# A fused gated-convolution kernel, forward and backward: order of the first slice, loading of k, buffers of gate and up, and replacement of the gradient pieces

## The chip, the cores and the metric

The kernel runs on one core of a Trainium2 chip. Its engines are TensorE (PE; its weight loads are listed as PEld), VectorE (DVE), ScalarE (ACT), GpSimd (POOL) and SyncE (SP). SP issues most of the transfers; ScalarE and GpSimd issue some too, each from its own instruction stream. The metric is the device time of one execution in microseconds. Before the change, nine runs have a median of 1946.38 us (1940.92 to 1960.81).

## The reference

All inputs are bf16. A sequence of 2048 rows by 1024 columns goes through a layer norm, and two branches use the result: a gated long convolution, and a bilinear unit with F = 3584. The kernel computes the output and the gradients of nine of the inputs (out_0 to out_9).

```python
xn = _layernorm(A_q)
# branch A: a short filter of 4 taps on k, times v, a long filter by FFT, gated by xn
k_shift = sum_t  k_pad[:, t:t + S, :] * shift_k[:, ks - 1 - t]
kv = k_shift * v
y  = irfft(rfft(kv, 2S) * rfft(ssm_k, 2S))[:S] + kv * ssm_D
s  = xn * y
# branch B
g = xn @ w_gate; u = xn @ w_up
g = silu((g * u) @ w_down)
out = A_q + s * g
# and the vector-Jacobian product of out with grad_out for
# q, k, v, shift_k, ssm_k, ssm_D, w_gate, w_up, w_down
```

## The kernel before, in words

The work runs in five stages, which one can tell by the line of TensorE's matmuls.

*Startup and forward.* `layer_norm` normalizes 2048 rows in six chunks and turns them into XNT (U0 to U3). `gu_unit(sl, b0, n, w, tick)` makes n blocks of 128 rows of gate and up for one slab of 256 columns of F: eight matmuls a block (L635), a copy from PSUM to `gut` by ScalarE (L637), a store of `gut` to GUd issued by ScalarE (L642), then the product hN on VectorE (L646), its store to Hd through GpSimd's queue, the turn of hN by TensorE (L656), a copy by ScalarE and a store to HTd. The pool `fg` has two buffers of `gut`.

Between the blocks lies the long convolution, `conv_forward`, a generator. `tick` counts blocks and calls `pump`, which runs the generator forward to a given fraction of `F_TOTAL`; that is how its work is dealt out among the matmuls. The convolution goes over eight slices of 128 columns. For each pair of slices `shift` makes kv from k (with a halo of three rows), v and the taps, on VectorE. k arrives in two steps: `copy_k` copies 256 columns of k to a scratch tensor KSLd through SP's queue (rows of its own, three zero rows ahead of them, written by `zero_rows`), and `cld_k` loads it from there, eleven rows for each partition in one piece, through GpSimd's queue. For each slice, `half` transforms kv and the filter by matmuls with the tables T4 (L235), ScalarE copies the result to SP tiles (L257, L295), and VectorE does the rest (`transform`): first kv's spectrum KX, then the filter's HX, their `product`, and the inverse. `h_rows` turns the filter's rows, which `load_h` puts into the first half of U5. From L778 on VectorE keeps the order in which the code issues (`PIN`).

*Gates.* L949 multiplies by w_down; `gate` makes the output and the gradients that go further back. *Weight gradients.* L1302 and L1319 by slabs, then L1395 for w_down, with h loaded from Hd by `load_h` (L1334); the backward convolution (`conv_backward`, which starts with the forward transforms of dy in `dy_forward`) is dealt out among these by `bpump` on VectorE.

*Input gradient* (L1447). The gradient of xn from branch B is a sum over 14 pieces n; a piece is `ts[n]`, 512 rows of dg or du in 128 x 4 x 512, loaded transposed by `load_dgut` (L1385) in two transposing transfers on SP's queue. The 16 row blocks make four groups of four. In the first group every piece is used for all four blocks; in the later ones two passes, b = 4g and 4g + 2, go over all pieces for two blocks each. Every pass fills two tiles `psx` of PSUM, of which there are four. `ln_backward` reads them on VectorE (L1478), goes on with the gradient through the layer norm, and stores a block of the result. In the same stage `dk_units` makes the gradients of k and of the taps on VectorE; it loads k and its gradient transposed (kT, dkT, L1119 and L1121) on SP's queue as well, and each of these has one buffer. The pieces of the next group go into the same buffers (`gd`, `gd2`, one each) as those being used.

Queues keep order: a transfer on SP that waits for TensorE or VectorE holds up those behind it.

Of the kernel before, what the change touches and what calls it, by code (L numbers as in the profile page):

```python
# [13 lines left out]
BF16 = mybir.dt.bfloat16  # L14
# [5 lines left out]
def build_kernel(  # L20
# [55 lines left out]
    def cld_k(t, c, dp):  # L76

        src = KSLd[dp]
        cld(t, bass.AP(src.tensor, src.offset + 1024 * c * 256, [[8 * 256, P], [256, 11], [1, 256]]))

# [21 lines left out]
    KSHd = dram.tile([4, P, NB, 256], BF16, name="KSHd")  # L102
    KSLd = dram.tile([4, S + 8, 256], BF16, name="KSLd")
    DYd = dram.tile([8, P, NB, P], BF16, name="DYd")
# [4 lines left out]
    GUd = dram.tile([NSL, 2, P, 2, 8, SLW], BF16, name="GUd")  # L109
    Hd = dram.tile([NSL, P, NB, SLW], BF16, name="Hd")  # L110
    HTd = [[dram.tile([n, S // 2], BF16, name=f"HTd{i}{n}") for n in (24 * P, 4 * P)] for i in range(2)]
# [23 lines left out]
    def zero_rows(bsb):  # L135
        zr = bsb.tile([8, 8, P], BF16, name="zr")
        V.memset(zr[:], 0.0)
        st(KSLd[:, 0:3, :], zr[0:4].rearrange("p a x -> p (a x)")[:, 0:768].rearrange("p (a x) -> p a x", a=3))
        st(DKSHd[:, S:S + 8, :], zr[:])
# [387 lines left out]
    Dz = kst.tile([P, D], BF16, name="Dz")  # L527
    V.memset(Dz[:], 0.0)
    bsb = pool("bc_sb", 1)
    tg = pool("tg", 1)  # L530
# [82 lines left out]
    def flush(age=0):  # L613
# [3 lines left out]
        while later and later[0][0] >= age:  # L617
            later.pop(0)[1]()

    hn = [nop]  # L620
    chunk = [0]

    def gu_unit(sl, b0, n, w, tick):

        if n == 4:
            gut = fg.tile([P, 2, 4, SLW], BF16, name="gut")
            hN = fg.tile([P, 4, SLW], BF16, name="hN", bufs=3)
        else:
            gut = lnp.tile([P, 2, 2, SLW], BF16, name="gut_s", bufs=6)
            hN = lnp.tile([P, 2, SLW], BF16, name="hN_s", bufs=6)  # L630
        for i in range(n):
# [12 lines left out]
        def multiply():  # L644
            with tc.issue_after(last.ins) if b0 + n <= 4 and chunk[0] <= 2 else nullcontext():
                tt(hN[:, 0:n], gut[:, 0, 0:n], gut[:, 1, 0:n], MUL)  # L646
            st(Hd[sl][:, b0:b0 + n, :], hN[:, 0:n])
            defer(turn)
        hn[0] = multiply

        def turn():
            hT = fg.tile([P, 2, 4, P], BF16, name="hT") if chunk[0] > 5 else lnp.tile([P, 2, 4, P], BF16, name="hT_s", bufs=5)
            ps = ps_tr.tile([P, 2, 4, P], BF16, name="tr")
            for a in range(2):
                for i in range(n):
                    nc.tensor.transpose(ps[:, a, i, :], hN[:, i, a * P:(a + 1) * P], ident[:])  # L656
            nc.scalar.copy(out=hT[:, :, 0:n], in_=ps[:, :, 0:n])
            fr, so = sl % 12 * SLW, b0 % 8 * P
            ld(HTd[b0 // 8][sl // 12][fr:fr + SLW, so:so + n * P].rearrange("(a f) s -> f a s", f=P),
               hT[:, :, 0:n].rearrange("f a i s -> f a (i s)"))  # L660

# [7 lines left out]
    def conv_forward():  # L669
        S_ = conv_state  # L670

        def load_kv(dp, c):
            if c == 0:
                S_["k", dp] = kst.tile([P, 2, 11, 256], BF16, name="k")
            cld_k(S_["k", dp][:, c], c, dp)
            v = U[4][:, 2048 * c:2048 * c + 2048].rearrange("p (a x) -> p a x", a=8)
            cld_v(v, c, dp * 256, 256)

# [104 lines left out]
        tl = turn_tables(ps_y)  # L783
        sp = [half(0, kvs(0), i) for i in range(2)]
        for ds in range(8):
            yield 0.5
            if ds % 2 == 1 and ds < 7:
                with tc.issue_after(S_["kst"].ins):
                    for c in range(2):
# [4 lines left out]
            HX = cs.tile([P, 16, 256], BF16, name="HX", bufs=2)  # L794
            room = HX[:].rearrange("p a x -> p (a x)").bitcast(F32).rearrange("p (a x) -> p a x", a=8)[:, 0:4]
            yield from transform(ds, 0, sp, KX, room, lambda i: sph.append(half(ds, S_["hx"], i, D0)), nop)
            S_["kst"] = st(KFd[ds], KX[:])
            next(tl, None)
            eight = (ds, 1) in EIGHT
            room = cf.tile([P, 4, 256], F32, name="room", tag="hx")[:] if eight else None  # L800
            yield from transform(ds, 1, sph, HX, room, nop1 if eight else lambda c: h_rows(ds + 1, c),
                                 lambda: next(tl, None))
            if eight:
                h_rows(ds + 1, 0)
# [40 lines left out]

    def copy_k(dp):
        ld(KSLd[dp, 3:3 + S, :].rearrange("(p a) d -> p a d", a=16),
           kin[:, dp * 256:(dp + 1) * 256].rearrange("(p a) d -> p a d", a=16))
    copy_k(0)
    ang, ang_ins = angles(tg)  # L850
# [43 lines left out]
    def tick(by=1):  # L894
        cnt[0] += by
        if cnt[0] == -2:
            pump((SHIFT_W + 3.95) / F_TOTAL)
        if cnt[0] >= 0:
            pump((SHIFT_W + (F_TOTAL - SHIFT_W) * (cnt[0] + 5) / (NT + 2)) / F_TOTAL)

    pump(SHIFT_W / F_TOTAL)
    for i_ in (4, 5):
        gu_unit(1, *xs[i_][0:2], slabs[1], tick)
    for sl in range(2, NSL - 2):
        w, wld = load_slab(sl, nc.sync)
        if sl in (2, 4, 6):
            with tc.issue_after(wld.ins):
                copy_k(sl // 2)
        for hf in range(2):
            for b0 in (8 * hf, 8 * hf + 4):  # L910
                gu_unit(sl, b0, 4, w, tick)
# [70 lines left out]
    def dy_forward(xs_, sp, cs, then):  # L982
# [10 lines left out]
        load(1)  # L993
        yield 7.0
        half(0, 0)
# [161 lines left out]

    C_TOTAL = 7.0 + 8 * FWD8_W + 16 * (PROD_W + INV8_W) + 8 * 1.4 + 8 * 2.5
    bpump, bdrain = make_pump(conv_backward(), C_TOTAL)
# [174 lines left out]
    def load_h(sl):  # L1334
        h = u8(HSL[sl % 3], "p (b f) -> p b f", b=NB)
        ld(h, Hd[sl])
        hs[sl] = h
# [46 lines left out]

    def load_dgut(g, n):  # L1385

        a, j = pieces[n]
        t = (gd2 if n < 4 else gd).tile([P, 4, 512], BF16, name=f"dgut{n}")
        for i in range(2):
            nc.sync.dma_start_transpose(out=t[:, 2 * i:2 * i + 2], in_=DGd[2 * j + i, a, 512 * g:512 * g + 512, :])  # L1390
        return t

    def dwd_mm(ps, h, f, dh):
        for b in range(NB):
            nc.tensor.matmul(ps, h[:, b, f * P:(f + 1) * P], DBM[b // 4][:, b % 4, dh * 512:(dh + 1) * 512],  # L1395
                             start=(b == 0), stop=(b == NB - 1))
# [101 lines left out]
    for n in range(12):  # L1498
        for i in range(4):
            dx_part(ts, i, pss[i], n)  # L1500
        ts[n] = load_dgut(1, n)
    for i in range(4):
        for n in (12, 13):
            dx_part(ts, i, pss[i], n)
        if i == 3:
            for n in (12, 13):
                ts[n] = load_dgut(1, n)
        with tc.high_priority(40):
            ln_backward(i, pss[i][:])
    for g in range(1, 4):  # L1510
        for b in (4 * g, 4 * g + 2):
            end = b == NB - 2
            pss = [ps_x.tile([P, D], F32, name="psx") for i in range(2)]
            for n in range(12 if end else 14):
# [5 lines left out]
                if end and n == 4:  # L1520
                    h = u8(2, "p (b f) -> p b f", b=NB)
                    ld(h, Hd[NSL - 1])
                if end and n == 8:
                    ln_loads(NB - 1)
                if b % 4 == 2 and not end:
                    ts[n] = load_dgut(g + 1, n)
            if end:
# [81 lines left out]
```

## Time and profile before

| | |
|---|---|
| median of nine runs | 1946.38 us (1940.92 to 1960.81) |
| the profiled execution | 1960.81 us, span 1959.0 us |
| TensorE busy | 1923.8 us, 98% |
| VectorE busy | 1543.8 us, 79% |
| ScalarE busy | 638.4 us, 33% |
| GpSimd busy | 310.0 us, 16% |
| mean granted TensorE clock | 0.995 |
| moved by DMA | 448.62 MB, mean 229 GB/s |

The profile is of one execution, and its time is one of the nine. A busy engine is one with an instruction running; transfers count for none of them. "Idle before" an instruction is the time that its engine stood still, with what ended that. The granted clock is the share of full speed that TensorE was given; where it is 0.50, a matmul takes twice as long. The timeline joins neighbouring instructions of the same kind (x16 is sixteen of them).

### The profile page before, as it was taken

How to read it: one execution, taken by the hardware profiler on the slowest of the kernel's cores; microseconds unless marked ns; L12 is line 12 of the kernel's file. 1: busy time of each engine (PE TensorE's matmuls, PEld its weight loads, DVE VectorE, ACT ScalarE, POOL GpSimd, SP SyncE). 2: the span in 40 equal slices, each digit the busy share in tenths (PEclk: the TensorE clock that was granted, in tenths of full speed). 3: DMA queues.
4: the chain of work that ended last, by engine and by line, in shares of the span. 5: the costliest groups of instructions: out<-in, count | busy, mean ns of one | idle time of the engine just before them, and what ended most of it. 6: DMA issues, size and time to landing. Idle time of an engine off the chain costs nothing.

```text
span 1959.0 us, 27347 instructions
## 1 busy us (share of the span) xinstructions
PE 1923.8 (98%) x10994; PEld 1033.6 (53%) x10994; DVE 1543.8 (79%) x1719; ACT 638.4 (33%) x942; POOL 310.0 (16%) x454
## 2 busy tenths in 40 slices
PE   8999999999999999999999999999999999998989
PEld 4555555555544447665666665654444444443434
DVE  9999999999837556887899999999994405677673
ACT  5854555555422224342222222222212002001122
POOL 4111111101112220001022221211212002111111
PEclk9999999999999999999999999999999999999999
DMA  9886856657879987656788697585889999897993
GB/s 311 283 262 220 285 200 211 233 205 253 285 221 315 306 281 269 220 203 213 265 249 265 219 265 257 180 281 176 244 221 193 138 203 224 145 182 157 192 197 131
DMA packets 457071, 448.62 MB, mean 229 GB/s; under 512 B 266916, under 2 KB 377576, under 8 KB 442480
## 3 DMA queue, kind: packets, MB, share of 16 engines
q1 hardware_dynamic: 401168, 247.55, 49.0%
q0 software_dynamic: 39456, 169.96, 26.9%
q10 hardware_dynamic: 16320, 29.36, 4.1%
q8 instruction: 86, 1.41, 0.3%
q14 instruction: 41, 0.34, 0.1%
HBM read 198.20 MB, written 189.84 MB: 198 GB/s over the span
## 4 chain that ended last, share of the span: by engine, by line
PE 72%; DVE 9%; DMA 7%; issue 3%; SPq 2%; ACT 1%; POOL 0%; DVEq 0%; ACTq 0%; POOLq 0%
PE psb L1319 20%; PE psb L1302 10%; PE psbm L949 10%; PE psb L1395 9%; PE psg L635 9%; PE psx L1447 8%; PE psF L235 3%; SPq L1390 2%; DMA GUd<-gut 1%; DVE W L213 1%; DVE dkp L1148 1%; DVE U L213 1%; DMA HTd<-hT 1%; DVE KX L213 1%; DMA xn_t<-XNd 1%
## 5 line engine op out<-in xcount | busy, mean ns | idle before, releaser
L635 PE MATMUL psg<-wslab,U 128*128 128x512 bf16 x1792 | 409.9, 380 | 5.2 <-ACT gut L637 2.7
L1319 PE MATMUL psb<-U,U 128*128 128x512 bf16 x1792 | 397.4, 379 | 0.0
L1447 PE MATMUL psx<-U,dgut 128*128 128x512 bf16 x1536 | 338.0, 382 | 10.8 <-DMA dgut<-DGd 10.8
L1447 PEld LDWEIGHTS <-dgut 128*128 128x128 bf16 x1792 | 176.0, 98 | 226.8 <-DMA dgut<-DGd 13.5
L1319 PEld LDWEIGHTS <-U 128*128 128x128 bf16 x1792 | 175.3, 98 | 197.5
L635 PEld LDWEIGHTS <-U 128*128 128x128 bf16 x1792 | 173.3, 98 | 192.2 <-issue 7.5
L1302 PE MATMUL psb<-wdt,U 128*128 128x256 bf16 x1792 | 205.3, 273 | 0.0
L1302 PEld LDWEIGHTS <-U 128*128 128x128 bf16 x1792 | 175.3, 98 | 30.7
L637 ACT CAST gut<-psg 128x512 bf16<-128x512 f32 x216 | 125.9, 587 | 182.5 <-PE psg L635 162.0
L1395 PE MATMUL psb<-U,U 128*128 128x512 bf16 x816 | 177.1, 379 | 0.0
L213 DVE TENSOR_TENSOR W<-W 128x1024 f32<-128x1024 f32 (+1 forms) x168 | 168.8, 1022 | 3.6
L1324 ACT CAST wb<-psb 128x512 bf16<-128x512 f32 x112 | 65.6, 585 | 311.1 <-PE psb L1319 292.7
L949 PE MATMUL psbm<-U,ht 128*128 128x512 bf16 x672 | 145.7, 379 | 0.0
L1395 PEld LDWEIGHTS <-U 128*128 128x128 bf16 x896 | 87.4, 98 | 104.6
L1479 ACT ACTIVATE dx_t<-dxn 128x1024 bf16<-128x1024 f32 x15 | 15.9, 1057 | 336.3 <-DVE dxn L213 336.3
L949 PEld LDWEIGHTS <-ht 128*128 128x128 bf16 x672 | 65.6, 98 | 78.6
L1304 ACT CAST dht<-psb 128x512 bf16<-128x512 f32 x112 | 65.5, 585 | 120.2 <-PE psb L1302 119.0
L213 DVE TENSOR_TENSOR U<-U,dht 128x2048 bf16<-128x2048 bf16 x56 | 68.2, 1220 | 44.7 <-ACT dht L1304 44.6
L213 DVE TENSOR_TENSOR dxn<-psx,dxna_t 128x1024 f32<-128x1024 f32 x15 | 18.3, 1222 | 98.6 <-PE psx L1447 84.4
L1148 DVE SCALAR_TENSOR_TENSOR dkp<-dkT,kT 128x1024 bf16<-128x1024 bf16 (+2 forms) x64 | 78.3, 1224 | 19.2 <-DMA dkT<-DKSHd 17.3
L1426 ACT CAST wbs<-psb 128x512 bf16<-128x512 f32 x51 | 29.9, 585 | 146.4 <-PE psb L1395 137.0
L213 DVE TENSOR_TENSOR W<-SP 128x1024 f32<-128x1024 f32 x64 | 74.2, 1218 | 2.9 <-ACT SP L295 2.4
(249 smaller groups left out, 2368.8 us busy)
## 6 DMA issues: line engine op xcount, KB each, us to landing
U<-GUd SPq DMA_DIRECT2D x28, 1024.0 KB, 7.8
DGd<-U SPq DMA_DIRECT2D x28, 1024.0 KB, 4.4
GUd<-gut ACTq DMA_DIRECT2D x54, 512.0 KB, 6.2
out_dram<-wb SPq DMA_DIRECT2D x112, 128.0 KB, 4.0
U<-Hd SPq DMA_DIRECT2D x14, 1024.0 KB, 5.7
Hd<-hN POOLq DMA_DIRECT2D x54, 256.0 KB, 5.3
HTd<-hT SPq DMA_DIRECT2D x52, 256.0 KB, 3.9
ht<-HTd SPq DMA_DIRECT2D x6, 1536.0 KB, 11.5
```

Of the source, the lines that this page charges most:

```text
L213: pinned(V.tensor_tensor(o, a, b, op))
L235: mm = nc.tensor.matmul(ps[:, k].rearrange("p (c d) -> p c d", c=2), T[:, r, k, :], xr[:, r], start=(n == 0), stop=(n == len(rs) - 1 and ( ...
L635: gu_mm[0] = nc.tensor.matmul(ps[:], XNT[q][:, dc, qi * P:(qi + 1) * P], w[:, dc].rearrange("p a f -> p (a f)"), start=(dc == 0), stop=(dc ...
L637: nc.scalar.copy(out=gut[:, :, i], in_=ps[:].rearrange("p (a f) -> p a f", a=2))
L949: mm = nc.tensor.matmul(ps[:, dh * 512:(dh + 1) * 512], ht(fc)[:, i * P:(i + 1) * P], WD[fc // 4][:, fc % 4, dh * 512:(dh + 1) * 512], sta ...
L1148: ins = V.scalar_tensor_tensor(prod[:].rearrange("p r d -> p (r d)")[:, lo:H], dkT[:, 0, lo:H], 1.0, kT[:, 0, 13 + m + lo:13 + m + H], op0 ...
L1302: nc.tensor.matmul(ps[:, x * SLW:(x + 1) * SLW], DBMT[2 * hf + g][:, dc, (b % 4) * P:(b % 4 + 1) * P], wdt[:, dc, :], start=(dc == 0), sto ...
L1304: nc.scalar.copy(out=dht[:, 2 * e:2 * e + 2].rearrange("p b f -> p (b f)"), in_=ps[:])
L1319: nc.tensor.matmul(ps[:], XN[b // 4][:, b % 4, dc * P:(dc + 1) * P], dgus[b // 8][:, :, b % 8], start=(b == 0), stop=(b == NB - 1))
L1324: nc.scalar.copy(out=wb[:, dc % 2].rearrange("p a f -> p (a f)"), in_=ps[:])
L1395: nc.tensor.matmul(ps, h[:, b, f * P:(f + 1) * P], DBM[b // 4][:, b % 4, dh * 512:(dh + 1) * 512], start=(b == 0), stop=(b == NB - 1))
L1447: nc.tensor.matmul(ps[:, dh * 512:(dh + 1) * 512], t[n][:, f, i * P:(i + 1) * P], WGU[n][:, f, dh * 512:(dh + 1) * 512], start=(n == 0 and ...
```

## The change

It has four parts and some edits that go with them.

1. *Forward, first slice.* The filter is transformed ahead of kv: `sp` is filled from hx, HX is made first (with KX as room), then KX. The pump is called earlier, so that `h_rows` stands ahead of the first unit after the startup.
2. *k.* `cld_k` reads k from the input itself, eleven rows of 512 bytes for each partition. The first half of the sequence takes three loads (partitions 16 to 127, 1 to 15, and 0, which has three rows less), since row -3 to -1 do not exist; they are set to zero once in a single tile `krow`, which all pairs of slices use. KSLd, `copy_k` and its calls go. For the first pair both halves of k are loaded ahead of both of v.
3. *gate and up.* Every third unit of four blocks puts `gut` into the second half of U5 (not in the last two slabs). hN and Hd hold the two halves of a slab's columns one after the other; the product reads `gut` in that order, and `dwd_mm` reads h in it.
4. *Gradient pieces.* `load_dgut` can load one half, 256 rows, into an existing tile. In groups 1 and 2 each pass asks, after each piece, for that half of the next group's piece whose columns this pass has just used. The first group's loads stay whole.

The backward convolution's first half is dealt out four units later (`yield 11.0`, `C_TOTAL`).

```diff
     def cld_k(t, c, dp):
-        src = KSLd[dp]
-        cld(t, bass.AP(src.tensor, src.offset + 1024 * c * 256, [[8 * 256, P], [256, 11], [1, 256]]))
+        rows = lambda u, n, a: bass.AP(kin.tensor, kin.offset + (1024 * c + 8 * u - 3 + a) * D + dp * 256,
+                                       [[8 * D, n], [D, 11 - a], [1, 256]])
+        for u, n, a in ((0, P, 0),) if c else ((16, P - 16, 0), (1, 15, 0), (0, 1, 3)):
+            cld(t[u:u + n, a:], rows(u, n, a))
...
+    krow = kst.tile([P, 2, 11, 256], BF16, name="k")
+    V.memset(krow[0:1, 0, 0:3, :], 0.0)
...
         if n == 4:
-            gut = fg.tile([P, 2, 4, SLW], BF16, name="gut")
-            hN = fg.tile([P, 4, SLW], BF16, name="hN", bufs=3)
+            turn_of[0] += 1
+            if turn_of[0] % 3 == 0 and sl < NSL - 2:
+                gut = U[5][:, 2048:4096].rearrange("p (a i f) -> p a i f", a=2, i=4)
+            else:
+                gut = fg.tile([P, 2, 4, SLW], BF16, name="gut")
+            hN = fg.tile([P, 2, 4, P], BF16, name="hN", bufs=3)
...
-                tt(hN[:, 0:n], gut[:, 0, 0:n], gut[:, 1, 0:n], MUL)
-            st(Hd[sl][:, b0:b0 + n, :], hN[:, 0:n])
+                by_half = lambda t: t.rearrange("p i (a f) -> p a i f", a=2)
+                tt(hN[:, :, 0:n], by_half(gut[:, 0, 0:n]), by_half(gut[:, 1, 0:n]), MUL)
+            st(Hd[sl][:, :, b0:b0 + n, :], hN[:, :, 0:n])
...
         def load_kv(dp, c):
-            if c == 0:
-                S_["k", dp] = kst.tile([P, 2, 11, 256], BF16, name="k")
-            cld_k(S_["k", dp][:, c], c, dp)
-            v = U[4][:, 2048 * c:2048 * c + 2048].rearrange("p (a x) -> p a x", a=8)
-            cld_v(v, c, dp * 256, 256)
+            S_["k", dp] = krow
+            if dp > 0 or c == 0:
+                for i in range(2) if dp == 0 else (c,):
+                    cld_k(krow[:, i], i, dp)
+            if dp > 0 or c == 1:
+                for i in range(2) if dp == 0 else (c,):
+                    v = U[4][:, 2048 * i:2048 * i + 2048].rearrange("p (a x) -> p a x", a=8)
+                    cld_v(v, i, dp * 256, 256)
...
-        sp = [half(0, kvs(0), i) for i in range(2)]
+        sp = [half(0, S_["hx"], i, Dz[:, 0:P]) for i in range(2)]
...
-            yield from transform(ds, 0, sp, KX, room, lambda i: sph.append(half(ds, S_["hx"], i, D0)), nop)
-            S_["kst"] = st(KFd[ds], KX[:])
+            own_room = lambda X: X[:].rearrange("p a x -> p (a x)").bitcast(F32).rearrange("p (a x) -> p a x", a=8)[:, 0:4]
+            eight = (ds, 1) in EIGHT
+            if ds == 0:
+                yield from transform(0, 1, sp, HX, own_room(KX), lambda i: sph.append(half(0, kvs(0), i)), nop)
+            else:
+                yield from transform(ds, 0, sp, KX, own_room(HX), lambda i: sph.append(half(ds, S_["hx"], i, D0)), nop)
+                S_["kst"] = st(KFd[ds], KX[:])
...
-        if cnt[0] == -2:
-            pump((SHIFT_W + 3.95) / F_TOTAL)
+        if cnt[0] == -4:
+            pump((SHIFT_W + 4.05) / F_TOTAL)
...
-    pump(SHIFT_W / F_TOTAL)
+    pump((SHIFT_W + 3.95) / F_TOTAL)
...
-        if sl in (2, 4, 6):
-            with tc.issue_after(wld.ins):
-                copy_k(sl // 2)
...
-        yield 7.0
+        yield 11.0
...
-    def load_dgut(g, n):
+    def load_dgut(g, n, t=None, h=None):
         a, j = pieces[n]
-        t = (gd2 if n < 4 else gd).tile([P, 4, 512], BF16, name=f"dgut{n}")
+        if t is None:
+            t = (gd2 if n < 4 else gd).tile([P, 4, 512], BF16, name=f"dgut{n}")
+        r0, r1 = (0, 512) if h is None else (256 * h, 256 * h + 256)
         for i in range(2):
-            nc.sync.dma_start_transpose(out=t[:, 2 * i:2 * i + 2], in_=DGd[2 * j + i, a, 512 * g:512 * g + 512, :])
+            nc.sync.dma_start_transpose(out=t[:, 2 * i:2 * i + 2, r0:r1], in_=DGd[2 * j + i, a, 512 * g + r0:512 * g + r1, :])
...
-                if b % 4 == 2 and not end:
-                    ts[n] = load_dgut(g + 1, n)
+                if g < 3:
+                    load_dgut(g + 1, n, ts[n], b % 4 // 2)
```

## The prediction

> **What bounds the kernel now.** I read the page first, then TensorE's waits, then busy time by stage, then the timeline around each gap.
>
> ```profile
> span 1959.0 us, 27347 instructions
> PE 1923.8 (98%) x10994; PEld 1033.6 (53%) x10994; DVE 1543.8 (79%) x1719; ACT 638.4 (33%) x942; POOL 310.0 (16%) x454
> ```
>
> TensorE is busy for 98% of the span, and the change leaves its 10994 matmuls as they are. Only idle TensorE time, and time at a lower clock, can be won. The busy time by stage (startup, forward, gates, weight gradients, input gradient) says where that lies; the columns are stretch, length, busy time of PE, PEld, DVE, ACT, POOL, granted clock, DMA share, GB/s.
>
> ```profile
> 0.00:60.00 60.00, 51.32 (x393) 29.88 (x394) 54.94 (x154) 35.35 (x56) 24.21 (x42) 1.00 0.95 325
> 60.00:500.00 440.00, 428.13 (x2647) 238.78 (x2646) 420.36 (x372) 248.31 (x347) 59.98 (x98) 0.99 0.70 235
> 500.00:733.00 233.00, 232.86 (x1164) 110.62 (x1163) 146.27 (x209) 69.94 (x81) 43.50 (x68) 1.00 0.92 284
> 733.00:1538.80 805.80, 805.74 (x4941) 472.25 (x4940) 691.04 (x664) 225.45 (x375) 125.13 (x151) 1.00 0.76 229
> 1538.80:1941.50 402.70, 391.86 (x1794) 175.99 (x1792) 223.49 (x314) 52.00 (x74) 56.04 (x94) 0.98 0.95 185
> ```
>
> TensorE idles 8.7 us in the startup, 11.9 in the forward stage, 10.8 in the input-gradient stage (L1447), and nothing to speak of between. The clock is below 1.00 in the same two later stages. Where:
>
> ```profile
> 1772.79 1.89 PE L1447 MATMUL psx<-U,dgut 128*128 128x512 bf16 x4 [2.60 <-DMA dgut<-DGd]
> 1776.49 4.97 PE L1447 MATMUL psx<-U,dgut 128*128 128x512 bf16 x16 [1.81 <-DMA dgut<-DGd]
> 1782.06 3.19 PE L1447 MATMUL psx<-U,dgut 128*128 128x512 bf16 x14 [0.59 <-DMA dgut<-DGd]
> ...
> 1876.99 7.21 PE L1447 MATMUL psx<-U,dgut 128*128 128x512 bf16 x22 [5.84 <-DMA dgut<-DGd]
> ...
> 191.71 3.27 PE L235 MATMUL psF<-kv,TF 128*128 128x256 bf16 x16 [2.27 <-DVE kv L213]
> ...
> 308.82 1.91 PE L235 MATMUL psF<-kv,TF 128*128 128x256 bf16 x16 [0.93 <-DVE kv L213]
> ...
> 353.77 1.89 PE L635 MATMUL psg<-wslab,U 128*128 128x512 bf16 x8 [1.26 <-ACT gut L637]
> ...
> 396.68 1.67 PE L635 MATMUL psg<-wslab,U 128*128 128x512 bf16 x7 [1.24 <-ACT gut L637]
> ```
>
> And what follows three of these gaps (same columns as above; the clock is the third number from the right):
>
> ```profile
> 192.06:195.47 3.41, 3.41 (x17) 2.23 (x15) 3.38 (x3) 1.46 (x2) 0.00 (x0) 0.50 0.48 192
> ...
> 1772.43:1779.26 6.83, 4.66 (x11) 1.48 (x12) 1.39 (x2) 3.17 (x5) 0.54 (x1) 0.50 1.20 206
> 1874.83:1881.66 6.83, 4.67 (x11) 1.65 (x12) 4.00 (x5) 2.50 (x5) 1.61 (x3) 0.50 1.22 214
> ```
>
> **The clock, row against rule.** After these gaps the clock stands at 0.50, so half of the busy time there is lost too: 1.7 us after the kv gap, 2.3 after each dgut gap. The Trainium skill (TensorE: Matmul & The Clock Gate, Part 1) says that the clock is halved after an idle window of about 3.4 us. Read as "a gap must last that long", only the 5.84 gap would cost clock, and the change would gain 1.7 + 2.3 = 4.0 us less. The trace halves it after 2.27 and 2.60 us. I take the row. A fourth halving at 492.4 (1.7 us) follows a wait that the change doesn't touch, so the stage sums are: startup 8.7, forward 11.9 + 3.4 = 15.3, input gradient 10.8 + 4.7 = 15.5, together 39.5 us.
>
> **Part 1: gradient pieces in halves.** A pass over two row blocks is 224 matmuls, 48.4 us at 0.216 each (112 in 24.34). Before, the pieces for the next group of four blocks are asked for only in the second pass: 28 transposes, each due 45 us after its piece is freed. The queue can't keep that: the 28 issues for the third group begin at 1697.6 and end at 1781.6, since each holds SP for 2.42 us on average (1.22 at best) and key transposes stand between them waiting for VectorE:
>
> ```profile
> 1697.61 25.68 SPq L1390 DMA_TRANSPOSE dgut<-DGd  x10
> 1728.35 1.19 SPq L1119 DMA_TRANSPOSE kT<-in_A_k_dram  x1
> ```
>
> After, a half (256 rows) is asked for in each pass and due 97 - 3 = 94 us later. The four waits are 0.6 to 5.8 us long against a notice of 45, so doubled notice covers them. The waits in the built order are per half, so no pass waits for the other half. *Rule against it:* DMA: Bandwidth & Descriptors (Latency and other measured facts) gives transposing DMAs 261 GB/s with a strided middle dimension. A 256 KB piece would take 1.0 us, 28 would be through in 28 us, and lateness would need another cause, for which halving is worth 0. The trace has 2.42 us, 108 GB/s; I take it.
>
> The price is issues: 112 half pieces instead of 56 whole ones. A half-size transpose isn't in the trace. Below it is half of 1.22 (0.6 us); above, the whole's own stretched 2.42. The nearest row is a whole at rest, 1.22 to 1.31; I take 1.0. A pass then holds SP 28 x 1.0 plus 3.5 key pairs x 2.5 = 37 us of 48.4. Gain: 15.5, the whole stage loss.
>
> What is late next is psx. VectorE frees it in an order fixed by its own chain, and it never waits for TensorE here. The last pass began at 1941.5 - 48.4 = 1893.1; without the stalls it begins at 1877.6 and its second block needs its bank at 1879.3. VectorE reads that bank here:
>
> ```profile
> 1880.31 1.23 DVE L213 TENSOR_TENSOR dxn<-psx,dxna_t 128x1024 f32<-128x1024 f32 x1
> ```
>
> It ends at 1881.5: 2.2 us late if VectorE's chain keeps its time. That chain will move both ways. In SP's new order, 14 halves stand ahead of the key transpose that came directly after the second group's pieces (1673.55), so it goes out 14 us later, and VectorE, which waited 7.8 us there, waits more. Its later waits for dkT, dxna_t, xn_t and the dka store from 1714 on sum to some 36 us, and arise in bursts of whole pieces which now spread over two passes; if half goes, 18 is won back. Net cost between 0 and 14; I take 1.
>
> **Part 2: the first slice's filter first.** VectorE ends kv at 74.7, then idles 1.58 and 2.39 us for the copies of kv's transform. The filter needs neither k nor v, so its copies are ready and VectorE gains 2.4 to 4 us. The kv gap (2.27 + 1.7 clock) and the 0.93 one end on VectorE, 95% busy in this stage, so a lead there shortens them: at most 4.9; at least the lead of 2.4. I take 4.9, because closing the 2.27 gap also spares the clock.
>
> **Part 3: third gate/up buffer.** ScalarE waits 17.7 us in 7 places for the store of gut; two reach TensorE, 1.26 + 1.24 = 2.5. The third buffer lies in the free half of U5, so nothing is queued behind it. Gain 2.5 (at least 0, if the store's own lateness grows).
>
> **Part 4: k's rows straight.** SP loses four copies through KSLd, POOL gains: loads of v (512 rows of 512 B) hold POOL 0.76 us, loads of 128 long rows 0.54, so 1408 rows cost 0.54 + 1280 x 0.22/384 = 1.27, and per slice pair four issues take 3.5 instead of 1.1 us. POOL is 16% busy: hidden. For the first pair the last k issue ends at 44.7 instead of 43.7; with its 10.3 us to landing that is 55.0, and VectorE reads it at 55.3. Cost 0 to 3 us (a late landing delays VectorE's whole forward chain); I take 0.5.
>
> **Edits at nothing.** hN as halves: 54 products at 684 ns; the same amount on 8 x 128 views (dkp<-dkh,Wbc) takes 680 to 690. Its store in 1 KB rows: POOL 0.54, hidden. The backward transform starts four units later, about 5 us: covered by VectorE's 42.3 us wait before the first dka at 1534; 5 without that cover.
>
> **Sum.** 15.5 + 4.9 + 2.5 - 1 - 0.5 = 21.4 us in the profiled execution: 1960.8 (span 1959.0 and 1.8 around it) to 1939.4. That execution is 14.4 us above the median of the nine. Which of the 39.5 us the median run lacks can't be seen. If all 14.4 lie in what is mended (22.9), 22.9 - 14.4 - 1.5 = 7.0 is left to gain: 1939.4. If none does, 1946.4 - 21.4 = 1925.0. In proportion (25.1/39.5), 0.635 x 22.9 - 1.5 = 13.0: **1933 us**, which I take.
>
> **Rivals.** (a) *The wait moves to psx.* The 14 us of key transposes aren't won back: the last passes wait for VectorE, and dgut's share, 15.5 x 0.635 = 9.8, is lost: 1943. For it: VectorE reads these banks 36 and 44 us after their pass has ended (1893.1 - 48.4 - 8.2 = 1836.5). Against: its DMA waits should shrink. (b) *The forward gain is used up by VectorE*, which has only 20 us of slack in 440: 0.635 x 7.4 = 4.7 is lost: 1938. Against: the gaps are short. (c) *Slower: SP becomes the bound.* If a half holds SP as long as a whole did, 112 x 2.42 + 12 key pairs x 2.5 = 301 us from 1673 end at 1974, while the last piece is due at 1922: 52 us of stalls, 1933 + 52 = 1985. It decides from 1.95 us a half on ((249 - 30)/112). For it: the 2.42 includes time for which bytes alone don't account. Against: pieces at rest take 1.3 and four-times pieces (U<-in_B_w_gate) 4.6, so size counts. (d) *The third buffer does nothing*, ScalarE waiting elsewhere: 1933 + 1.6.
>
> **How the numbers follow.** The forecast, with (d), 0.58: 1925 to 1939; (a) 0.18; (b) 0.12; (c) 0.12. About 0.5% (9.7 us, 1936.7) is what a measurement of this kernel tells from no change. Four fifths of the forecast's span lie below that: 0.47 faster. The rest of it, (a) and (b): 0.41 the same. (c): 0.12 slower. The range, 1925 to 1947, holds all but (c) and some of (a)'s tail.
>
> **What would show it.** Right: no wait of psx matmuls for dgut, clock 1.00 from 1540 on, the half transposes near 1 us on SP, no kv gap near 190, no gut gap near 352 and 396. Wrong: TensorE waiting for VectorE's dxn at the head of the last pass (a), kv gaps that remain or move (b), L1404 holding SP for about 2 us each and dgut waits in several passes (c), or VectorE starting its first product on k later than 55.3.

## The result, and the profile after

The changed kernel takes 1935.95 us (median of 18 runs, 1933.46 to 1941.25) against 1946.36 us (55 runs, 1936.56 to 1962.89): a ratio of 0.9943 with a 95% interval of 0.9926 to 0.9959, or 10.4 us. The profiled execution took 1935.35 us. That is within the range and near the predicted 1933. But the runs below show that this was largely luck: the parts that were to bring the gain bring little or nothing in them, and an edit that was put at nothing brings 3.1 us.

The page after, first the span and the busy times, then the stages (stretch, length, busy time of PE, PEld, DVE, ACT, POOL, granted clock, DMA share, GB/s):

```profile
span 1933.6 us, 27507 instructions
PE 1917.3 (99%) x10994; PEld 1033.2 (53%) x10994; DVE 1543.0 (80%) x1720; ACT 639.0 (33%) x942; POOL 329.7 (17%) x461
```
```profile
0.00:60.00 60.00, 53.81 (x398) 31.34 (x399) 55.76 (x155) 36.01 (x57) 27.04 (x43) 1.00 0.91 301
60.00:500.00 440.00, 433.94 (x2710) 243.63 (x2709) 426.56 (x380) 253.69 (x354) 74.21 (x105) 1.00 0.70 235
...
1538.80:1925.00 386.20, 386.20 (x1791) 175.05 (x1789) 217.64 (x302) 56.86 (x82) 53.74 (x91) 1.00 0.90 189
```

TensorE now idles 6.1 us in the forward stage (11.9 before) and not at all in the input gradient up to 1925 (10.8 before). TensorE's longest waits in the forward stage, from the table of waits (us in total, times, longest):

```profile
PE psF L235 <- DVE kv L213: 3.2, 2, 2.3
PE psF L235 <- ACT SP L257: 0.6, 2, 0.3
PE tr L726 <- ACT hx L729: 0.6, 1, 0.6
```

The waits for gut near 352 and 396 are gone, as forecast. Both waits for kv are there, as long as before (2.27 and 0.93 us). And one loss is gone that the prediction had left out of the change's reach: before, TensorE idled 3.7 us between 470 and 493, with 1.7 us lost to the halved clock after it; after, it idles 0.3 us there.

Where the profiled executions differ can be put into three numbers for each, all from TensorE's timeline: when the gates begin (first L949 or L957 matmul), how long from there to the first psx matmul, and from there to the end of the span.

| execution | gates begin | to the input gradient | to the end |
|---|---|---|---|
| before | 534.3 | 1004.3 | 420.3 |
| after | 524.5 | 1004.7 | 404.4 |

The difference is 9.8 us in startup and forward stage and 15.9 in the input gradient. These three numbers are used for the experiments too.

### The profile page after: what moved, and what is told of

It is laid out like the page before. It is cut to its first block, busy times and chain, and to the rows that moved or that the text cites. A ratio compares the mean times of both kernels' runs of the same rounds, so it can differ in the third digit from the quotient of the medians.

```text
span 1933.6 us, 27507 instructions
## 1 busy us (share of the span) xinstructions
PE 1917.3 (99%) x10994; PEld 1033.2 (53%) x10994; DVE 1543.0 (80%) x1720; ACT 639.0 (33%) x942; POOL 329.7 (17%) x461
## 4 chain that ended last, share of the span: by engine, by line
PE 89%; DVE 7%; ACT 1%; issue 1%; DMA 1%; SPq 0%; DVEq 0%; ACTq 0%
PE psb L1331 20%; PE psx L1461 20%; PE psg L642 13%; PE psb L1314 10%; PE psbm L961 10%; PE psb L1409 9%; PE psF L235 3%; DVE W L213 2%; DVE U L213 1%; DVE KX L213 1%; PE psY L438 1%; PE tr L669 1%; PE psY L449 1%; PE psY L1108 1%; DVE bst L556 1%
## 5 line engine op out<-in xcount | busy, mean ns | idle before, releaser
L1461 PE MATMUL psx<-U,dgut 128*128 128x512 bf16 x1536 | 332.8, 379 | 0.0
L644 ACT CAST gut<-psg 128x512 bf16<-128x512 f32 x156 | 91.1, 587 | 129.2 <-PE psg L642 127.2
L1493 ACT ACTIVATE dx_t<-dxn 128x1024 bf16<-128x1024 f32 x15 | 15.9, 1057 | 322.6 <-DVE dxn L213 322.6
L66 POOL DMA_DIRECT2D Hd<-hN x54 | 37.0, 685 | 265.2 <-DVE hN L213 262.3
```

The costliest lines, as they stand in the source:

```text
L644: nc.scalar.copy(out=gut[:, :, i], in_=ps[:].rearrange("p (a f) -> p a f", a=2))
L1461: nc.tensor.matmul(ps[:, dh * 512:(dh + 1) * 512], t[n][:, f, i * P:(i + 1) * P], WGU[n][:, f, dh * 512:(dh + 1) * 512], start=(n == 0 and ...
```

## Experiments

Each time stands beside runs of the kernel before on the same chip, which was not always the same chip. On all of these chips the kernel before was quicker than in the runs above: 1941.1 to 1941.3 us in place of 1946.4. The first three rows of the table come from one chip, the next three and the change itself from a second, the other three from a third. Rows of different chips are compared by their ratios, whose intervals are some 3 us wide to either side; on the second chip differences of 1 to 2 us can't be told either.

| kernel | median, us | ratio to before, 95% |
|---|---|---|
| halves alone | 1941.15 | 0.9993 (0.9977 to 1.0009) |
| change without halves | 1935.98 | 0.9969 (0.9953 to 0.9985) |
| change without third buffer | 1935.66 | 0.9966 (0.9949 to 0.9982) |
| change, kv first | 1935.68 | 0.9968 (0.9955 to 0.9980) |
| change, k through KSLd | 1935.76 | 0.9962 (0.9946 to 0.9978) |
| change, old layout of hN and Hd | 1938.67 | 0.9977 (0.9961 to 0.9993) |
| change, old layout, no third buffer | 1937.99 | 0.9973 (0.9955 to 0.9990) |
| new layout of hN and Hd alone | 1938.08 | 0.9979 (0.9959 to 0.9999) |
| change itself | 1935.53 | 0.9960 (0.9942 to 0.9978) |
| change, kv's transform later | 1934.39 | 0.9949 (0.9930 to 0.9968) |

The theory at the start was the prediction's: the halves are the largest part of the gain. The rival was that the dgut waits belong to the profiled execution of before.

**Before, profiled again**

> The kernel before, unchanged, profiled a second time. The first profiled execution lay 14 us above the median of its runs. Theory (the loss of an execution varies where a transfer is late): the kv gaps of 2.27 and 0.93 us are the same to 0.1 us, since no transfer is in them; the dgut waits differ, and an execution near 1946 us has 5 to 10 us of them with their clock instead of 15.5. Rival (the whole program is slower in some executions): the dgut waits are again 10 to 11 us, and the time is spread over all stages.

It took 1941.71 us, and its span is 1939.9. The waits of TensorE from 60 us on:

```profile
PE psF L235 <- ACT SP L295: 3.4, 3, 2.4
PE psF L235 <- DVE kv L213: 3.2, 2, 2.3
PE psg L635 <- ACT gut L637: 1.5, 2, 0.8
PE tr L712 <- ACT hx L715: 1.3, 2, 1.1
```

There is no wait for dgut at all, not even the 5 to 10 us that the theory left. The three numbers are 531.3, 1004.3 and 404.3: the input gradient takes as long as after the change. What this execution loses lies in the forward stage.

**The halves alone**

```diff
-                if b % 4 == 2 and not end:
-                    ts[n] = load_dgut(g + 1, n)
+                if g < 3:
+                    load_dgut(g + 1, n, ts[n], b % 4 // 2)
```

> The kernel before with one part of the change: the gradient pieces are asked for in halves, one half in each pass. Theory: this is the largest part of the gain; the waits for dgut (10.8 us and 4.7 us of halved clock in the profiled execution) go, and in the median run about 0.635 of that, less 0 to 3 us for the longer wait for dkT: 1936 to 1940 us, 0.9950 to 0.9965 of before. TensorE's waits for kv and for gut in the forward stage stay as before. Rival (the dgut waits are a matter of the profiled execution alone, and the gain lies in the forward stage): 1944 to 1947 us, no difference from before.

1941.15 us against 1941.33: no gain. The three numbers are 532.0, 1004.3 and 404.3, those of before without its dgut waits. The theory's 1936 to 1940 falls.

**The change without halves**

The same lines the other way round, in the changed kernel.

> The changed kernel with whole gradient pieces, asked for in the second pass, as before. Theory: the dgut waits come back and cost what the halves had won, 6 to 10 us in the median: 1942 to 1946 us; the forward stage keeps its shortened waits. Rival (the waits were an accident of timing that any shift of the stage removes): 1935 to 1938 us, as the changed kernel.

1935.98 us: level with the changed kernel, with no wait for dgut (524.2, 1004.7, 404.4). On this chip no worth of the halves shows in either direction. What they do is seen on SP's queue. One line each from the view of the dgut transposes between 1640 and 1900 (duration min, median, max in ns), without halves and then in the changed kernel:

```profile
L1404 SPq DMA_TRANSPOSE dgut<-DGd x62: 1223/1418/8317, 1638.1 to 1856.1; - x62
```
```profile
L1404 SPq DMA_TRANSPOSE dgut<-DGd x119: 1191/1215/5109, 1640.3 to 1855.2; - x119
```

A half holds SP for 1.2 us, as a whole does at its best. Twice the instructions would thus cost SP twice its time if none were stretched. Here fewer halves are stretched than wholes: in the mean a half takes 1.36 us and a whole 2.04, so that the same bytes cost SP 1.3 times the time. A half lands 4.1 us after its issue in the median, a whole 5.8.

**Without the third buffer**

```diff
-            turn_of[0] += 1
-            if turn_of[0] % 3 == 0 and sl < NSL - 2:
-                gut = U[5][:, 2048:4096].rearrange("p (a i f) -> p a i f", a=2, i=4)
-            else:
-                gut = fg.tile([P, 2, 4, SLW], BF16, name="gut")
+            gut = fg.tile([P, 2, 4, SLW], BF16, name="gut")
```

> The changed kernel without the third buffer for gate and up. Theory: ScalarE waits for the store of gut again at six or seven places (about 17 us), of which 2.5 us reach TensorE near 352 and 396, and the stall of TensorE between 474 and 492 us (3.7 us idle and 1.7 of halved clock before, 0.31 after) comes back as well, since ScalarE is behind there: 4 to 8 us slower than the changed kernel, 1940 to 1944 us. Rival (the stall near 480 went because of another part): 2.5 us or less, 1936 to 1938.5 us and no stall near 480.

1935.66 us: no loss. The theory's 1940 to 1944 falls; the rival is right about the stall, and its 1936 to 1938.5 lies just above the time. TensorE waits at most 0.4 us at a time for gut, and 0.3 us near 480; ScalarE waits 4.9 us for stores of gut between 60 and 500 (17.7 and 6.7 in the two executions of before). Its profiled execution, 1943.0, is the slowest of its twelve: TensorE waited 4.2 us for dbm at 724 there, with 6.8 us of halved clock (1011.5 for the middle number). That shows again how little one execution says about a wait that comes and goes.

**kv first, and k through KSLd**

The first undoes the new order of the first slice and the new points of the pump; the second brings back `copy_k` and the loads from KSLd.

```diff
-        sp = [half(0, S_["hx"], i, Dz[:, 0:P]) for i in range(2)]
+        sp = [half(0, kvs(0), i) for i in range(2)]
...
-        if cnt[0] == -4:
-            pump((SHIFT_W + 4.05) / F_TOTAL)
+        if cnt[0] == -2:
+            pump((SHIFT_W + 3.95) / F_TOTAL)
```

> The changed kernel with the first slice's order as before (kv's transform first, the pump at its old points); k's rows, the third buffer and the halves stay. After the first four runs (halves alone: no gain; without halves or without the third buffer: all of it) the gain of some 6 us in the median must come from the filter's order, k's rows or the layout of the products. Theory 1 (the order of the first slice carries it): 1940 to 1942 us, with the stall of 3.4 us between 470 and 487 and its halved clock back. Theory 2 (it lies in k's rows or in the layout of Hd): 1935 to 1937 us, no stall there; startup and forward stage lose 0 to 1.5 us.

> The changed kernel with k copied through KSLd again (four more copies of 1 MB each on SP, contiguous loads on POOL). Theory 1 (k's rows carry the gain): 1940 to 1942 us, the stall between 470 and 487 back. Theory 2 (they cost or bring nothing, as taken with 0.5): 1934.5 to 1937 us; the last copy lies near slice 6 (170 us), far ahead of 470.

1935.68 and 1935.76 us beside 1935.53 for the changed kernel on the same chip: neither order nor loading of k moves the time by more than the 1 to 2 us that these runs can tell. In both executions the gates begin at 522.6 and 522.7, 2.5 us earlier than in the changed kernel's beside them (525.2); 1.7 us of that is that the clock was not halved after the kv gap in these two, on which more below.

**The old layout of hN and Hd, and the change itself**

Left were the "edits at nothing". Undone was the layout in halves of 128 columns:

```diff
-    Hd = dram.tile([NSL, P, 2, NB, P], BF16, name="Hd")
+    Hd = dram.tile([NSL, P, NB, SLW], BF16, name="Hd")
...
-                by_half = lambda t: t.rearrange("p i (a f) -> p a i f", a=2)
-                tt(hN[:, :, 0:n], by_half(gut[:, 0, 0:n]), by_half(gut[:, 1, 0:n]), MUL)
-            st(Hd[sl][:, :, b0:b0 + n, :], hN[:, :, 0:n])
+                tt(hN[:, 0:n], gut[:, 0, 0:n], gut[:, 1, 0:n], MUL)
+            st(Hd[sl][:, b0:b0 + n, :], hN[:, 0:n])
```

> The changed kernel with the products hN and their DRAM copy Hd in the layout before (runs of 2 KB, not two runs of 1 KB). Theory 1 (the layout carries the gain: the stores of gut and Hd land in 10.3 and 7.9 us before and in 8.0 and 7.0 after, between 455 and 486, so that the store of hT which ends the stall comes 3 us earlier): 1940 to 1942 us, the stall back. Theory 2 (more and shorter runs can only cost): 1935 to 1936.5 us, no stall.

> The changed kernel itself, beside the three above on one chip. If the halves matter only where the pieces come late, it is level with the kernel without halves: 0.9965 to 0.9972 of before on a chip whose before is near 1941, 0.994 on one near 1946.

1938.67 us beside 1935.53: 3.1 us slower (1.8 to 4.3 at 95%, by resampling the twelve runs of each), the only part whose absence shows. The time lies between the ranges of the two theories, and the changed kernel's ratio, 0.9960, just below the range that was expected for it. The gates begin at 527.8 instead of 525.2. In the profiled execution the stall is back, 3.19 us idle and 3.4 us at half clock (1.7 us lost); but here the clock was not halved after the kv gap, so the two executions differ by less than the stall. TensorE in the old layout:

```profile
478.85 1.89 PE L642 MATMUL psg<-wslab,U 128*128 128x512 bf16 x8
483.93 0.60 PE L235 MATMUL psF<-hx,TF 128*128 128x256 bf16 x4 [3.19 <-ACT SP L295]
```

The chain behind it, from ScalarE's timeline of the kernel before (second execution):

```profile
480.65 0.59 ACT L637 CAST gut<-psg 128x512 bf16<-128x512 f32 x1 [1.14 <-PE psg L635]
485.42 1.01 ACT L657 COPY hT<-tr 128x1024 bf16<-128x1024 bf16 x1 [4.19 <-DMA HTd<-hT]
486.33 0.59 ACT L637 CAST gut<-psg 128x512 bf16<-128x512 f32 x1
486.81 1.95 ACT L295 COPY SP<-psF 128x1024 f32<-128x1024 f32 x2
```

The same copy in the changed kernel (second execution):

```profile
480.12 1.01 ACT L670 COPY hT<-tr 128x1024 bf16<-128x1024 bf16 x1 [1.43 <-DMA HTd<-hT]
```

Before, ScalarE stands 4.19 us at the copy of hT, because the store that last read this buffer has not landed; behind it stand the copies of gut and SP that free TensorE's banks. That store was issued on SP at 465.71, behind two loads of w_down of 1 MB each and one of HTd, and landed 19.6 us later. So the stall depends on how fast the DMA engines get through this burst. The DMA view of 18 us from the first load of w_down on (packets, MB, share of the 16 engines' time; q0 is GpSimd's queue, here with the stores of Hd; q1 is SP's), kernel before first:

```profile
DMA packets 4883, 5.35 MB, mean 297 GB/s; under 512 B 145, under 2 KB 3214, under 8 KB 4880
...
q1 hardware_dynamic: 4169, 3.73, 71.7%
...
q0 software_dynamic: 167, 0.54, 12.0%
```

and the changed kernel's second execution:

```profile
DMA packets 5967, 5.92 MB, mean 329 GB/s; under 512 B 153, under 2 KB 4295, under 8 KB 5964
...
q1 hardware_dynamic: 5255, 4.30, 79.0%
...
q0 software_dynamic: 160, 0.52, 7.7%
```

The same half megabyte of Hd takes 12.0% x 16 x 18 = 34.6 us of engine time before and 22.2 us after, 64 and 43 us for a MB. SP's queue moves 4.30 MB in place of 3.73 in the same time, and ScalarE waits 1.4 us for the store of hT in place of 4.2. The 0.57 MB more cost SP's queue some 30 us of engine time at its 53 us for a MB. Of these, 12 come from the store of Hd; the rest comes from other bytes that cost less as well (SP's own 53 us for a MB in place of 55, ScalarE's queue 15.4% in place of 16.9% for the same 1.05 MB) and from a slightly higher busy share. Why those got cheaper too is not shown.

**The new layout alone**

The same edit put into the kernel before.

> The kernel before with one edit of the change: hN and Hd in halves of 128 columns, the store in runs of 1 KB. Theory (after the run with the old layout was 3.1 us slower than the changed kernel, and runs without each other part were level with it): this edit carries the gain; the stall at 470 to 487 with its halved clock goes (5 us of TensorE), the store of Hd takes some 0.7 of the DMA time per byte, and the time is 1935.5 to 1938 us, 0.9970 to 0.9983 of a before near 1941.3. Rival (the layout works only beside the third buffer, which takes 6.7 to 17.7 us of ScalarE's waits away): 1939 to 1941.5 us, the stall still there in part.

1938.08 us against 1941.14, ratio 0.9979 (0.9959 to 0.9999): 3.1 us again, about half of the change's gain on these chips (1941.32 - 1935.53 = 5.8). The DMA view of the same stretch:

```profile
DMA packets 5841, 5.86 MB, mean 326 GB/s; under 512 B 151, under 2 KB 4154, under 8 KB 5838
...
q0 software_dynamic: 164, 0.52, 7.8%
```

The layout alone brings the rate. In the same stretch of all 14 profiled executions, the five with the old layout have 11.0 to 12.0% and 297 to 302 GB/s, the nine with the new one 7.7 to 8.5% and 322 to 336 GB/s, whatever else differs. The stall is down to 1.13 + 0.32 us, without a halved clock. It is not gone (ScalarE still waits 2.87 us for the store of hT), and gut's wait at 352 is still 1.70 us: theory and rival each hold in part, and the time lies just past the theory's 1938.

**Old layout and no third buffer**

> The changed kernel with the old layout of hN and Hd and without the third buffer. Theory (the two edits mend the same lateness of stores, so the third buffer is worth nothing beside the new layout and something beside the old): 1939.5 to 1941.5 us, 1 to 3 us over the run with the old layout alone, with gut gaps near 352 and 396 back. Rival (the third buffer is worth nothing in either): 1938 to 1939.3 us.

1937.99 us, level with the old layout alone (1938.67): no worth of the third buffer shows beside either layout, as the rival had it. There are 1.0 + 1.4 us of stall between 469 and 486, and ScalarE waits 2.86 us for the store of hT, as long as in the new layout alone, though the engines move 302 GB/s here and 326 there: the rate is not all that sets this wait. There are no gut gaps near 352 and 396, though the buffer is gone. But these gaps come and go by themselves: in the three executions whose forward part is that of before they are 1.26 and 1.24 us, 0.81 and 0.70, and 0.39 and none. What takes them away is not shown.

**kv's transform later**

In the second and fourth slice both transforms of the next kv are asked for one step later in the inverse.

```diff
+            late = ds in (1, 3)
-            yield from (inv8 if ds in INV8 else inv_dft)(KX, HX, cs, ahead, ahead)
+            yield from (inv8 if ds in INV8 else inv_dft)(KX, HX, cs, nop if late else ahead, ahead)
+            if late:
+                ahead()
```

> The changed kernel with kv's transforms of the third and fifth slice asked for one step later in the inverse (both halves, 2.4 to 5 us of VectorE's work later in TensorE's order). Theory (the waits for kv, 2.27 and 0.93 us, are set by where TensorE's order has these transforms, not by how early VectorE starts): both go and with the first the halved clock where it came, 1931 to 1933 us, 2 to 4 us faster than the changed kernel. Rival (VectorE, 97% busy there, now waits for the transform itself, and gives the time back at the next wait): 1934.5 to 1937 us.

1934.39 us. The trace shows the mechanism as expected; these are TensorE's waits from 60 to 530, its longest ones:

```profile
PE psg L642 <- ACT gut L644: 1.7, 1, 1.7
PE psF L235 <- ACT SP L257: 1.2, 3, 0.6
PE tr L726 <- ACT hx L729: 0.6, 1, 0.6
```

Both waits for kv are gone, and with them any halved clock in this stage; the gates begin at 521.6 (524.5 and 525.2 in the changed kernel's two executions). The median lies between the theory's range and the rival's: part of the gain is given back, in a wait of 1.7 us for gut at 518, where the changed kernel waits 0.6 in one of its two executions and not at all in the other. In the time it is 1.1 us ahead of the changed kernel's 1935.53, measured on another chip, and the two ratios' intervals overlap: that it is the faster of the two is not shown by the times, though it has the lowest ratio in the table. This execution also waited 2.94 us for dgut at 1664, with the halves in place.

**Quarters**

```diff
-        r0, r1 = (0, 512) if h is None else (256 * h, 256 * h + 256)
+        r0, r1 = (0, 512) if h is None else (128 * h, 128 * h + 128)
...
-                    load_dgut(g + 1, n, ts[n], b % 4 // 2)
+                    for q in (0, 1):
+                        load_dgut(g + 1, n, ts[n], b % 4 + q)
```

> The changed kernel with the gradient pieces in quarters of 128 rows, two after each piece in each pass: 56 transposing DMAs a pass instead of 28. Theory (each holds SP for some 1.22 us whatever its size, as the halves did): 56 x 1.22 = 68 us and 8 for the key transposes in a pass of 48.4, so SP is the bound: over four passes it falls some 110 us behind a notice of about 94, and the stage waits 20 to 110 us for dgut: 1955 to 2045 us. Rival (a piece holds SP in proportion to its size, 0.6 us for a quarter): 56 x 0.6 = 34 us, no wait, 1935 to 1937 us.

2048.49 us in one run. The view of the dgut transposes between 1640 and 1900, then what TensorE and VectorE waited for from 1536 on:

```profile
L1404 SPq DMA_TRANSPOSE dgut<-DGd x170: 1167/1196/4785, 1639.8 to 1899.6; - x170
```
```profile
PE psx L1461 <- DVE dxn L213: 98.3, 8, 32.3
```
```profile
DVE dkp L1160 <- DMA dkT<-DKSHd: 152.1, 10, 39.6
```

A quarter holds SP for 1.20 us, like a half and a whole. SP is the bound, but TensorE's matmuls do not wait for a piece even once. The key transposes stand in the same queue, VectorE waits 152 us for them, and TensorE waits for VectorE to read psx. That is rival (c)'s cause with rival (a)'s place. Idle time of 98 us, and a mean clock of 0.71 to 0.88 in the stretches from 1720 on, make the 112 us over the changed kernel's span (1934.3 in its second execution).

## Why the prediction came out where it did

Of the predicted 13.0 us, 9.8 were to come from the halves, 3.1 from the filter's order and 1.6 from the third buffer (0.635 of each), less 1.5. On the later chips the halves alone bring 0.2 us, and taking out any one of the three costs nothing that shows. The median came out near all the same; with these mechanisms that is luck, unless the halves do bring more on the chips of the first comparison, which is open.

**What bounds the kernel.** Right in kind: only idle TensorE time and clock could be won. Wrong in weight, because the losses of one execution were taken for those of the kernel.

**Part 1, 15.5 us, and the step "in proportion".** In the first pair of executions the 15.5 are real: the last stretch went from 420.3 to 404.4 us. But of the four profiled executions with whole pieces, one waited for dgut, and of the ten with halves or quarters one (2.9 us). In a run like these others the input gradient has nothing to win. The step that failed is the last of the sum: that 14.4 us between the profiled execution and the median could not be located, and a share of 0.635 of every loss was kept. All of the dgut loss was missing in the second execution of before (1941.71). Had 14.4 been taken out of what is mended, as one of the two ends of that step had it, 7.0 would have been left, near the 5.8 measured on the later chips, though still with the wrong parts in it. The queue time was off too: a half was taken at 1.0 us for lying below a whole, and it is 1.2. The wait for dkT that 14 halves ahead of it would lengthen to 21.8 came out at 23.6. VectorE's later waits for transfers, some 36 us from 1714 on, of which half was to be won back, came down to 12; but they are only 21 in the second execution of before, which has no halves. Rival (a) did not come to pass: TensorE never waits for VectorE there.

**Part 2, 4.9 us: nothing.** The step that failed is the lead of 2.4 to 4 us that VectorE was to gain at 77 us: it did not arise. VectorE's timeline before and after the change, at the place where kv's copies had held it up, and then after the change just ahead of the kv gap:

```profile
72.41 2.29 DVE L213 TENSOR_TENSOR kv<-U,U 128x4096 bf16<-128x4096 bf16 x1
76.28 0.69 DVE L213 TENSOR_TENSOR hN<-gut 128x1024 bf16<-128x1024 bf16 x1 [1.58 <-ACT gut L637]
79.36 4.68 DVE L213 TENSOR_TENSOR W<-SP 128x1024 f32<-128x1024 f32 x4 [2.39 <-ACT SP L295]
```
```profile
77.38 0.69 DVE L213 TENSOR_TENSOR hN<-gut 128x1024 bf16<-128x1024 bf16 x1 [3.77 <-ACT gut L644]
77.99 1.22 DVE L213 TENSOR_TENSOR W<-SP 128x1024 f32<-128x1024 f32 x1
```
```profile
185.14 2.29 DVE L213 TENSOR_TENSOR U<-U,U 128x4096 bf16<-128x4096 bf16 x1
187.35 0.68 DVE L213 TENSOR_TENSOR hN<-gut 128x1024 bf16<-128x1024 bf16 x1
187.95 2.28 DVE L213 TENSOR_TENSOR kv<-U,U 128x4096 bf16<-128x4096 bf16 x1
```

The two waits of 1.58 and 2.39 became one of 3.77 for the next gut. VectorE is 1.4 us earlier at 78 and at 188, but so is TensorE at the gap (188.0 in place of 189.4; in the second execution of before, without the change, it is there at 187.7). Run with kv first, the changed kernel has waits of 1.40 and 2.40 there, 3.80 in all against 3.77. VectorE keeps its order, and the products hN in it wait for ScalarE's copies of what TensorE makes, so that it did not run ahead; the kv gap is the distance between kv's product in VectorE's order and kv's transform in TensorE's. The run with the later transform supports that: only moving it removed the gap of 2.27. Rival (b) was right that the gain would not come, though not by its cause: there was no lead to use up.

**Part 3, 2.5 us.** The gaps are not there after, and the buffer is not what the time hangs on: without it nothing is lost that shows. Rival (d) was right for the time. For ScalarE it did what was said (waits of 17.7 and 6.7 us in the two executions of before, none in the first after, 4.9 in the changed kernel without it).

**Part 4, cost 0.5.** Undone, it leaves the time where it is (1935.76 beside 1935.53), and VectorE's first product on k starts at 54.1, not later than 55.3. Right as far as these runs tell.

**Edits at nothing.** Here was the largest part that the runs show. hN in halves was costed on VectorE (684 ns, right) and GpSimd (0.54 us an issue, now 0.68, still hidden). The term that failed is the store of Hd, put at nothing for its issue time on GpSimd alone. That the layout changes what this store costs the DMA engines was not asked, although their busy share stood near its highest where the store of hT was late (1.08 to 1.10 between 465 and 480 in the second execution of before, by the stage view). The stall it shortens, 3.7 us with 1.7 of clock, was listed among the losses and left out of the change's reach: "follows a wait that the change doesn't touch" was wrong.

**Rival (c).** It was given 1.95 us a half as its point of decision, and the halves stayed at 1.2 us in the median and 1.4 in the mean. With quarters the same arithmetic (56 x 1.2 + 8 = 75 us in a pass of 48.4) crosses it, and the loss comes.

**What stays open.** The 10.4 us of the first comparison against 5.8 on the later chips. Of the 55 runs of before there, 18 lie above 1950 us, and none of the 18 runs of the changed kernel lies above 1941.3; on the later chips 1 of 29, 2 of 33 and 1 of 27 runs of before did. It would fit that dgut comes late more often there and that halves help then, but no run shows it. Of the 5.8 us the layout makes 3.1; for the other 2.7 no single part is shown, since undoing any one of the other four costs nothing that shows. In the traces they lie ahead of the gates: with the layout alone the gates begin at 527.6, in the changed kernel at 525.2, and the former still has 1.70 us of wait for gut at 352 and 1.45 of the stall. The later start of the backward convolution was undone in no run; the stretch it lies in takes 1004.7 us with it and 1004.3 without, so it brings nothing there. And why runs of 1 KB cost the engines less than runs of 2 KB was not tried. The Trainium skill (DMA: Bandwidth & Descriptors, Latency and other measured facts) tells of transfers that lose rate where the rows of the 128 partitions lie large powers of two apart in memory, with figures for 512 KiB to 8 MiB; here they lie 8 KB apart in both layouts, so that no run here bears on it.

## What to carry to other kernels

Profile the kernel before more than once before a loss is put into a sum: waits on VectorE in program order came back to 0.1 us, late transfers worth 15.5 us did not come back at all. When the layout of a store changes, look at its share of the DMA engines' time where they are full, and at what lands last behind it. Cutting a transposing transfer into smaller pieces is paid for in instructions on the issuing queue: from 256 KB down to 64 KB a piece cost the same 1.2 us here at its best, while one of 1 MB took 4.2. And whoever else uses that queue may pay first: with quarters it was VectorE, not TensorE.

## What the hardware showed that was not expected

*A price per transpose.* SP is held 1.22 us at least (median 1.42) by a transposing transfer of 512 rows, or 256 KB, 1.19 (1.22) by one of 256 rows and 1.17 (1.20) by one of 128.

*A layout's price on the DMA engines.* 64 against 43 us of engine time for a MB, with nearly the same number of packets (167 and 160), while the engines were full.

*The clock after equal gaps.* The kv gap of 2.27 us is the same in 13 profiled executions; in eight the clock was halved after it for 3.41 us, in five it was not. Two examples, each with the window that holds the gap and the next (columns as in the stages above), the changed kernel and then the change without halves:

```profile
187.43:190.84 3.41, 1.14 (x9) 0.68 (x8) 3.41 (x3) 0.58 (x1) 1.23 (x2) 1.00 0.73 269
190.84:194.25 3.41, 3.41 (x16) 2.10 (x14) 3.38 (x3) 1.86 (x2) 0.00 (x0) 0.50 0.50 192
```
```profile
189.42:192.83 3.41, 1.48 (x14) 1.32 (x14) 3.41 (x2) 0.69 (x2) 0.65 (x1) 1.00 0.99 380
192.83:196.25 3.42, 3.42 (x19) 1.71 (x18) 3.38 (x4) 2.11 (x3) 0.00 (x0) 1.00 0.24 81
```

All changes of the clock in an execution lie a multiple of 3.413 us apart. That agrees with what the Trainium skill (TensorE: Matmul & The Clock Gate, Part 1) says of a free-running window of 3413 ns, and it orders the 13 cases: lay such windows back from the last change of the clock, and the eight have 2.15 to 2.28 us of the gap inside one window, while in the five the gap lies across a border with at most 1.62 to 1.94 us in one. In the fences above the changed kernel has 1.14 us busy in the window with the gap, the other 1.48. Over all 14 profiled executions, from 60 us on, with the idle time as the trace records it (the ends of matmuls in it are modelled), every window at full clock with 2.15 us or more of idle TensorE was followed by a halved one, none with 1.7 or less was, and of those between (1.80 to 1.94) one of five was. The longest gap without a halving is the 2.94 us for dgut in the run with the later transform: a border splits it into 1.40 and 1.55. So a gap's place counts besides its length. The prediction took the halving after 2.27 us as certain (1.7 us each time); it came 8 times in 13.
